# A Fourier layer with two mixtures on one Trainium2 core: where the small tiled products of a group stand, and the forward spectra's way to TensorE

## Chip, core and metric

The kernel runs on one NeuronCore of a Trainium2 chip. The metric is the device time of one execution in microseconds (us). The kernel before has a median of 1930.59 us over three runs (1930.12 to 1937.83).

## What is computed

Input x is 8 batches of 3072 tokens with 256 features. Three layers follow one another, all in fp32:

```
X = rfft(x, axis=1)                         # along the tokens
Yr = Xr @ w_r - Xi @ w_i + b_r ; Yi = Xr @ w_i + Xi @ w_r + b_i
Y = soft_threshold(Yr, 0.01) + 1j * soft_threshold(Yi, 0.01)
y = irfft(Y).reshape(24576, 256)
logits = y @ phi                            # 32 slots = 8 experts x 4
d = softmax(logits, axis=0) ; c = softmax(logits, axis=1)
slot_out[e] = relu((d.T @ y)[e] @ w1[e]) @ w2[e]
z = c @ slot_out
h = z @ w_in ; out = (h * tanh(softplus(h))) @ w_out      # 256 -> 2048 -> 256
```

## The kernel before

The work has two stages. The first, some 650 us, does the Fourier layer, the logits, both softmaxes and the sum of tokens into slots. The second runs the experts on 32 slots and then the last layer over all tokens; the diff doesn't touch it.

The transform is split in steps. Stage one (`stage1`, L186) multiplies a batch by a 64-point table in 64 x 64 tiles of the array and stores the result to DRAM (`sdr`, L216). `load_b` (L218) brings it back in another order, a quarter of a batch at a time: such a quarter is a group, 8 frequencies q of the 32, and 8 batches make 32 groups k. Stage two (`stage2`, L224, tile `s`, 32 products per group) finishes the spectrum and splits it into a high and a low part. `linear` (L247) does the complex product by the weights in six runs of six products (tile `l`: two feature halves `eh`, three partial sums `m`); behind each run with m > 0, VectorE adds (`p`), ScalarE makes two one-sided thresholds (`cl`, in one buffer, and `p`), and GpSimd subtracts them into `yt` (L285).

From yt, three things are made. `project` (L290, tile `pp`, in 32-column tiles of the array) multiplies by phi in the frequency domain. `inv1` (L301, tile `iu`, also 32-column tiles) starts the inverse transform of these logits. `ytrans` (L313, tile `tr`) transposes yt, twelve times a group, for the later sum into slots; its operand takes every sixth float of yt. Once a batch, the softmax chain follows: `sturn`, `inv2` (`lps`), `smax1` to `smax3` (`mt`, `mb`: a maximum over all tokens, spread by a product with a 32-row matrix of ones), `csoft1`, `cexp`, `csoft2`, `ctrans` (`ctps`). `fwd1` (L425, tile `dps`) transforms the exponentials forward; for all batches but the last it stores the result (`dm`) to DRAM (`ddr`), and `d_load` (L442) loads it back as `dd`. The last batch is turned on chip instead, by VectorE and eight transposes (`td`). `fwd2` (L472, tile `dt`, 32-column tiles) makes the spectra, `dturn` (L482) turns them, and `slots` (L487, tile `sps`, 32-column tiles) adds up the slots.

The order is written out as numbers. `at(position, function, ...)` collects calls; a position counts groups, so k + 0.5 lies in the middle of group k. The calls are sorted and issued in that order, on all engines, the DMA queue of SyncE among them. The dictionary `PA` (L798) holds the offsets: stage one's six pieces of a batch stand at 4b - 5.89 + 0.3402 j for j = 1, 3 to 11, `project` stands at k + 1.18, `inv1` at k + 1.48, `ytrans` at k + 2.24, stage two at k - 1.1, `load_b` at k - 1.91, and the chain of batch b at 4b + 4 plus its own offset.

All along, `conv` (L529) turns the last layer's weights from 64-bit to 32-bit floats in 32 pieces, on VectorE and GpSimd. The last batch has positions of its own (`TAIL`).

At the start, loads fill the time; 36 products `wm` on the identity matrix (`warm`, L520) run before the first stage two.

Of the kernel before, what the change touches and what calls it, by code (L numbers as in the profile page):

```python
# [31 lines left out]
def constants():  # L32

    n1 = np.arange(R1, dtype=np.float64)
    n2 = np.arange(R2, dtype=np.float64)
    f1 = np.zeros((R1, R1))
    t = np.zeros((96, NP, 96))
    w = 2.0 * np.pi / SEQ
    f1[:, 0], f1[:, 1] = 1.0, np.where(n1 % 2 == 0, 1.0, -1.0)
    for pos in range(47):  # L40
        k, r = (R1 * (pos + 1), 0) if pos < 23 else (R1 // 2 + R1 * (pos - 23), R2)
        a = w * np.mod(n2 * k, SEQ)
        t[r:r + R2, 0, pos] = np.cos(a)
        t[r:r + R2, 0, 48 + pos] = -np.sin(a)
    t[0:R2, 0, 47] = 1.0
    t[0:R2, 0, 95] = np.where(n2 % 2 == 0, 1.0, -1.0)
    for q in range(1, NP):
        ang = 2.0 * np.pi * np.mod(n1 * q, R1) / R1
        f1[:, 2 * q], f1[:, 2 * q + 1] = np.cos(ang), -np.sin(ang)
        for k2 in range(R2):  # L50
            a = w * np.mod(n2 * (q + R1 * k2), SEQ)
            sg = 1.0 if k2 < R2 // 2 else -1.0
            t[0:R2, q, k2] = np.cos(a)
            t[R2:96, q, k2] = np.sin(a)
            t[0:R2, q, 48 + k2] = -sg * np.sin(a)
# [13 lines left out]
def body(ctx, tc, x, w_r, w_i, b_r, b_i, phi, w1, w2, w_in, w_out, cbig, ct, out, dbg=None, stop=False):  # L69
# [39 lines left out]
    t_t = tall[:, NP * 144:].rearrange("p (n f) -> p n f", f=96)  # L109
    ones32 = const.tile([NS, 128], F32, name="ones32")  # L110
    s_acc = const.tile([128, D], F32, name="s_acc")
# [13 lines left out]
    x_t, b_t, xh_t, xl_t, yt_t, y_t, pt_t, k1_t = {}, {}, {}, {}, {}, {}, {}, {}  # L125
    sdr, spt, ddr, ch, a_t = {}, {}, {}, {}, {}
    XC = 512
# [96 lines left out]
    def stage2(k, h, p0):  # L224
# [17 lines left out]
        if g == 0 and p0 == 0:  # L242
            for t in (xh_t[k], xl_t[k]):
                nc.vector.tensor_copy(t[:, h, 3 * NC:3 * NC + 48].rearrange("p (a r) -> p a r", r=2),
                                      t[:, h, 95:144:48][:, None, :].to_broadcast([128, 24, 2]).bitcast(F32))

    def linear(k, eh, m):  # L247
        if eh == 0 and m == 0:
            pool, tag = (bp, "b") if k >= NK - 2 else (yq, "yq") if k >= NK - 4 else (ytp, "yt")
            yt_t[k] = pool.tile([128, 2, 8, 2, 48], F32, tag=tag, name="yt")  # L250
        xh, xl, yt = xh_t[k], xl_t[k], yt_t[k]
# [15 lines left out]
        if m == 0:  # L267
# [6 lines left out]
            return  # L274
        ri = m - 1
        p = lp.tile([128, 8, 48], F32, tag="p", name="p")
        nc.vector.tensor_add(p.rearrange("p q f -> p (q f)"), ps, k1_t[eh][:, 0:NC])  # L277
        cl = lp.tile([128, 8, 48], F32, tag="cl", bufs=1, name="cl")
        if k == NK - 1:
            nc.vector.tensor_scalar(cl, p, tlo[:, ri, eh:eh + 1], thi[:, ri, eh:eh + 1], op0=ALU.max, op1=ALU.min)  # L280
            nc.vector.tensor_sub(yt[:, eh, :, ri, :], p, cl)
        else:
            nc.scalar.activation(out=cl, in_=p, func=AF.Relu, bias=tup[:, ri, eh:eh + 1])  # L283
            nc.scalar.activation(out=p, in_=p, func=AF.Relu, scale=-1.0, bias=tlo[:, ri, eh:eh + 1])  # L284
            nc.gpsimd.tensor_sub(yt[:, eh, :, ri, :], cl, p)  # L285
# [67 lines left out]
    def smax2(b):  # L353
# [209 lines left out]

    def s1pos(b, j):
        if b < 2:
            return -5 + 0.05 * j if b == 0 else 0.15 + 0.195 * j
        if b == 2:
            return 2.5 + 0.305 * j
        return 4 * b + PA["s1"] + PA["s1d"] * j

# [4 lines left out]
    for b in range(NB):  # L575
        for i in range(na // 2):
            at(s1pos(b, 2 * i + 1), stage1, b, i)
        for i in range(na // 2 if b else 0):
            at(s1pos(b, 2 * i + 1.5), store_a, b, i)
            at(s1pos(b, 2 * i - 2.4) if i > 1 else s1pos(b - 1, 2 * i + 9.6) if b > 1 else -3.86 + 0.01 * i, load_x, b, i)  # L580
    for k in range(NK):
# [13 lines left out]
    for b in range(NB):  # L595
# [378 lines left out]
```

## Time and profile before

| | |
|---|---|
| median of three runs | 1930.59 us |
| the profiled execution | 1935.8 us |
| its span, first to last instruction | 1934.0 us |
| TensorE busy | 1875.3 us, 97% of the span |
| VectorE, ScalarE, GpSimd busy | 1163.1, 860.5, 195.3 us |
| chain that ended last, by engine | PE 88%, DMA 4%, DVE 3%, ACT 2% |
| moved by DMA | 164.28 MB in 96,905 packets, 28,784 of them under 512 bytes |

In the profile PE is TensorE's products, PEld its weight loads, DVE VectorE, ACT ScalarE, POOL GpSimd and SP SyncE. The ends of products are modelled, so starts are what to compare. A product in fp32 has two records, a transpose one, and an l product (rounded fp32) one.

### The profile page before, as it was taken

The page shows a single profiled execution, that of the slowest core. Times are in us where ns is not written, and L with a number is a line of the kernel's source. Part 1 is how long each engine was busy: PE and PEld are TensorE (multiplying, and loading weights), DVE is VectorE, ACT ScalarE, POOL GpSimd, SP SyncE. Part 2 cuts the span into 40 slices and gives each one's busy share as a digit, 9 for nine tenths or more (in the row PEclk, how much of TensorE's full clock was granted, in tenths as well). Part 3 has the DMA queues.
Part 4 walks back from the last instruction along what each step waited for, and adds up shares of the span by engine and source line. Part 5 has one row for each costly group of instructions (what it writes and reads, how often), then busy time and mean ns, then how long its engine had stood idle before and what let it go on. Part 6 is the DMA issues. An engine that isn't in the chain of part 4 may idle for free.

```text
span 1934.0 us, 29831 instructions
## 1 busy us (share of the span) xinstructions
PE 1875.3 (97%) x12106; PEld 1569.4 (81%) x12106; DVE 1163.1 (60%) x1810; ACT 860.5 (44%) x1380; POOL 195.3 (10%) x247
## 2 busy tenths in 40 slices
PE   6899999998998899999999999999999999999999
PEld 4687787777887488888888888888888888888887
DVE  3355655655566476666666666666666666666665
ACT  2666666665754243333333333333333333333332
POOL 0333333332332000000000000000000000000000
PEclk9999999999999999999999999999999999999999
DMA  9867777775663920020020020002002001000000
GB/s 246 235 150 173 168 184 177 170 185 132 161 167 107 343 74 22 23 55 22 12 55 23 23 55 23 23 12 55 22 23 55 22 19 48 22 23 22 23 22 23
DMA packets 96905, 164.28 MB, mean 85 GB/s; under 512 B 28784, under 2 KB 58096, under 8 KB 94848
## 3 DMA queue, kind: packets, MB, share of 16 engines
q1 hardware_dynamic: 93808, 155.13, 29.2%
q0 software_dynamic: 1792, 4.76, 0.8%
q10 hardware_dynamic: 1168, 2.49, 0.5%
q8 instruction: 95, 1.56, 0.3%
q14 instruction: 42, 0.34, 0.1%
HBM read 98.78 MB, written 63.57 MB: 84 GB/s over the span
## 4 chain that ended last, share of the span: by engine, by line
PE 88%; DMA 4%; DVE 3%; ACT 2%; issue 2%; POOL 1%; SPq 0%; POOLq 0%; ACTq 0%; DVEq 0%
PE o L910 56%; PE h L868 9%; PE l L265 8%; PE s L233 6%; PE tr L318 2%; PE s L201 2%; DMA dd<-ddr 2%; DMA bt<-sdr 1%; PE pp L296 1%; DMA xc<-in_x_dram 1%; PE sps L496 1%; POOL yt L285 1%; PE dt L478 1%; ACT cl L283 1%; PE iu L307 1%
## 5 line engine op out<-in xcount | busy, mean ns | idle before, releaser
L910 PE MATMUL o<-whl,gh 128*128 128x512 f32 x3072 | 1082.9, 395 | 0.0
L910 PE MATMUL o<-whl,gl 128*128 128x256 f32 x3072 | 827.9, 280 | 0.0
L881 ACT ACTIVATE g<-h 128x1024 f32<-128x1024 f32 (+1 forms) x385 | 394.2, 1025 | 747.8 <-PE h L868 738.0
L910 PEld LDWEIGHTS o<-whl,gh 128*128 128x128 f32 x3072 | 566.5, 188 | 121.5
L910 PEld LDWEIGHTS o<-whl,gl 128*128 128x128 f32 x3072 | 578.5, 188 | 31.5
L894 DVE TENSOR_TENSOR gl<-g,gh 128x1024 fp32r<-128x1024 f32 x383 | 468.9, 1224 | 29.2 <-DVE gh L887 1.4
L887 DVE CAST gh<-g 128x1024 fp32r<-128x1024 f32 (+1 forms) x385 | 265.8, 690 | 352.6 <-ACT g L881 352.6
L868 PE MATMUL h<-ctt,mst 128*128 128x512 f32 x768 | 240.7, 394 | 1.5 <-ACT g L881 1.0
L233 PE MATMUL s<-tall,bt 96*128 96x144 f32 x1024 | 143.0, 301 | 23.0 <-DMA bt<-sdr 12.1
L233 PEld LDWEIGHTS s<-tall,bt 96*128 96x128 f32 x1024 | 138.6, 202 | 31.0 <-issue 26.4
L241 DVE TENSOR_TENSOR xl<-s,xh 128x432 fp32r<-128x432 f32 (+1 forms) x192 | 94.6, 550 | 113.6 <-ACT xh L240 113.3
L285 POOL TENSOR_TENSOR yt<-cl,p 128x384 f32<-128x384 f32 x124 | 125.2, 1010 | 352.6 <-ACT p L284 220.2
L868 PEld LDWEIGHTS h<-ctt,mst 128*128 128x128 f32 x768 | 121.0, 188 | 19.7 <-ACT g L881 1.8
L283 ACT ACTIVATE cl<-p,tup 128x384 f32<-128x384 f32 x124 | 76.3, 615 | 134.0 <-DVE p L277 98.1
L918 DVE TENSOR_TENSOR os<-o,os 128x256 f32<-128x256 f32 x192 | 76.5, 419 | 77.2 <-ACT os L917 77.2
L277 DVE TENSOR_TENSOR p<-l,k 128x384 f32<-128x384 f32 x128 | 70.6, 553 | 85.2 <-PE l L265 61.9
L240 ACT ACTIVATE xh<-s 128x432 fp32r<-128x432 f32 (+1 forms) x192 | 79.0, 503 | 36.7 <-PE s L233 36.3
L917 ACT ACTIVATE os<-o 128x256 f32<-128x256 f32 x192 | 73.4, 383 | 41.5 <-PE o L910 37.7
L284 ACT ACTIVATE p<-p,tlo 128x384 f32<-128x384 f32 x124 | 76.3, 615 | 4.0
L201 PE MATMUL s<-xc,f 64*64 64x512 f32 x384 | 56.6, 650 | 9.6 <-DMA xc<-in_x_dram 9.5
L318 PEld LDWEIGHTS tr<-cb,yt 128*128 128x128 f32 x384 | 55.4, 235 | 12.0 <-issue 4.5
L318 PE MATMUL tr<-cb,yt 128*128 128x128 f32 x384 | 62.2, 306 | 0.0
(187 smaller groups left out, 1392.1 us busy)
## 6 DMA issues: line engine op xcount, KB each, us to landing
sdr<-a SPq DMA_DIRECT2D x96, 256.0 KB, 3.8
bt<-sdr SPq DMA_DIRECT2D x32, 768.0 KB, 8.5
out_dram<-os SPq DMA_DIRECT2D x47, 512.0 KB, 2.6
xc<-in_x_dram SPq DMA_DIRECT2D x90, 256.0 KB, 5.4
ctt<-c_d SPq DMA_DIRECT2D x28, 384.0 KB, 7.0
w1t<-in_moe_w_dram SPq DMA_DIRECT2D x6, 1024.0 KB, 7.4
c_d<-chl SPq DMA_DIRECT2D x14, 384.0 KB, 2.8
w2t<-in_moe_w_dram SPq DMA_DIRECT2D x5, 1024.0 KB, 12.2
```

The source lines that it names most:

```text
L201: nc.tensor.matmul(ps[h][64 * c:64 * c + 64], lhsT=f64[hs], rhs=t[hs, XC * c:XC * c + XC], start=True, stop=True, tile_position=(64 * h, 6 ...
L233: nc.tensor.matmul(ps[:, i], lhsT=b_t[k][:, p0 + i, h * 128:(h + 1) * 128], rhs=t_m[:, 8 * g + p0 + i, :], start=True, stop=True)
L241: nc.vector.tensor_sub(part(xl_t[k]), ps, xh.bitcast(F32))
L265: nc.tensor.matmul(full[:, 0:48 * nq].rearrange("p (q f) -> p q f", f=48), lhsT=ww[:, h, es], rhs=spec(xx, h), start=n == 0, stop=n == 5)
L283: nc.scalar.activation(out=cl, in_=p, func=AF.Relu, bias=tup[:, ri, eh:eh + 1])
L285: nc.gpsimd.tensor_sub(yt[:, eh, :, ri, :], cl, p)
L318: nc.tensor.transpose(ps[:, i, eh], yt[:, eh].rearrange("p q r f -> p (q r f)")[:, 2 * c + i::6], ident)
L868: nc.tensor.matmul(ps[:, i], lhsT=mst[:, f * 128:f * 128 + 128], rhs=ct_t[b][:, 4 * m:4 * m + 4].rearrange("p n t -> p (n t)"), start=True ...
L881: nc.scalar.activation(out=v(g), in_=v(h), func=AF.Mish)
L887: nc.vector.tensor_copy(v(gh), v(g))
L894: nc.vector.tensor_sub(gl, g, gh.bitcast(F32))
L910: nc.tensor.matmul(o, lhsT=a[:, i, ts], rhs=w, start=f == 0 and n == 0, stop=f == 15 and n == 1)
```

## The change

- yt gets the layout [feature half, 6, 128] instead of [half, 8, 2, 48], so that the 128 columns of one transpose lie side by side. GpSimd's subtraction now takes its inputs with a step of six floats and writes runs of eight. The inverse table's rows are permuted to fit.
- `inv1` moves from k + 1.48 to k + 2.179, just ahead of the next group's `project`. The whole chain of a batch moves about 0.7 group later, `slots` a whole one.
- Stage one gets new positions by hand, most at 0.175 of a group, just ahead of `inv1` and `project`; its store follows 0.17 later.
- `fwd2`'s four parts stand together, just ahead of `project`.
- All batches take the last batch's way for the spectra: `dm` is turned by VectorE, then by eight transposes `td`, and copied into one tile `dd`. The DRAM tensor `ddr`, its store and its load are gone.
- The matrix of ones has 128 rows instead of 32 in the product `mb`.
- Behind the warm-up, 26 more products (`filler`, 9728 columns) run on a weight tile.

```
-    tt = t.transpose(2, 1, 0)
+    r = np.arange(16)
+    tt = t.transpose(2, 1, 0)[np.concatenate([6 * r + m for m in range(6)])]
...
-    ones32 = const.tile([NS, 128], F32, name="ones32")
+    ones32 = const.tile([128, 128], F32, name="ones32")
...
+    def split6(t):
+        return t.rearrange("p q (f m) -> p m q f", m=6)
...
-            yt_t[k] = pool.tile([128, 2, 8, 2, 48], F32, tag=tag, name="yt")
+            yt_t[k] = pool.tile([128, 2, 6, 128], F32, tag=tag, name="yt")
...
+        o = yt[:, eh].rearrange("p m (q r f) -> p m q r f", q=8, r=2)[:, :, :, ri]
...
-            nc.gpsimd.tensor_sub(yt[:, eh, :, ri, :], cl, p)
+            nc.gpsimd.tensor_sub(o, split6(cl), split6(p))
...
-            v = yt[:, eh].rearrange("p q r f -> p q (r f)")
+            v = yt[:, eh].rearrange("p m (q j) -> p q m j", q=8)
...
-                nc.tensor.matmul(ps[32 * a:32 * a + 32], lhsT=ph[:, eh, :], rhs=v[:, :, 32 * a:32 * a + 32],
+                nc.tensor.matmul(ps[32 * a:32 * a + 32], lhsT=ph[:, eh, :], rhs=v[:, :, 2 * a:2 * a + 2],
...
-                nc.tensor.transpose(ps[:, i, eh], yt[:, eh].rearrange("p q r f -> p (q r f)")[:, 2 * c + i::6], ident)
+                nc.tensor.transpose(ps[:, i, eh], yt[:, eh, 2 * c + i], ident)
...
-            if last:
-                nc.vector.transpose(out=dm.rearrange("p q n -> p n q")[:, 12 * i:12 * i + 12], in_=ps)
-            else:
-                nc.scalar.activation(out=dm[:, 12 * i:12 * i + 12], in_=ps, func=AF.Copy)
-        if last:
-            ch[b, 0] = dm
-            return
-        ddr[b] = dram.tile([NP, 96, NS], F32, tag="ddr", bufs=2, name="ddr")
-        nc.sync.dma_start(out=ddr[b].rearrange("q (r n) s -> (q r) n s", r=4), in_=dm)
+            nc.vector.transpose(out=dm.rearrange("p q n -> p n q")[:, 12 * i:12 * i + 12], in_=ps)
+        ch[b, 0] = dm
...
         if b < NB - 1:
-            dd = cp.tile([96, NP, NS], F32, tag="dd", name="dd")
-            nc.sync.dma_start(out=dd, in_=ddr[b].rearrange("q p s -> p q s"))
-            ch[b, 0] = [dd[:, q] for q in range(NP)]
-            return
+            both = cp.tile([96, 2, 4, 128], F32, tag="dd", name="dd")
...
+    def filler():
+        ps = psum([128, 512], "wm")
+        w = wsp["a"][0]
+        for m, n, c in ((128, 512, 5), (127, 512, 5), (64, 512, 4), (128, 256, 4), (127, 256, 4), (128, 128, 4)):
+            for _ in range(c):
+                nc.tensor.matmul(ps[0:m, 0:n], lhsT=w[:, 0, 0:m], rhs=w.rearrange("p h e -> p (h e)")[:, 0:n], start=True, stop=True)
...
+    S1 = {0: [-4.95 + 0.1 * i for i in range(6)], 1: [0.475, 0.84, 1.175, 1.475, 1.84, 2.175], 2: [2.475, 3.175, 4.175, 4.475, 5.175, 5.475]}
+    for b in range(3, NB):
+        S1[b] = [4 * b + z for z in PA["s1"]]
...
-        at(k + PA["pj"] + 0.3, inv1, k)
+        at(k + PA["pj"] + (0.999 if k < NK - 1 else 0.3), inv1, k)
...
-            at(f2 + 0.1 * g if b < NB - 1 else NK + TAIL["f2"][g], fwd2, b, g)
+            at(f2 + 0.001 * g if b < NB - 1 else NK + TAIL["f2"][g], fwd2, b, g)
...
-PA = dict(y=20, s1=-5.89, s1d=0.3402, lb=-1.91, s2=-1.1, pj=1.18, yt=2.24, tu=0.482, i2=1.17, m1=1.17, m2=1.34, m3=1.51, f1=1.84, c1=1.58, ce=1.58, ds=2.47, dl=2.05, c2=2.57, f2=2.46, sl=3.2, cx=3.24, ...)
+PA = dict(y=20, s1=(-5.825, -4.825, -4.525, -3.825, -2.825, -2.525), lb=-1.91, s2=-1.1, pj=1.18, yt=2.24, tu=1.185, i2=1.87, m1=1.87, m2=2.04, m3=2.21, f1=2.52, c1=2.28, ce=2.28, ds=3.29, dl=2.88, c2=3.27, f2=3.176, sl=4.19, cx=3.95, ...)
```

What this does to the order shows at two places. On TensorE, around the forward spectra `dt` of batch 2, first before, then changed (of each run of six l products the first row stands):

```order
L201 MATMUL s_3349<-xc,f_120 64x512 x2
L201 MATMUL s_3350<-xc,f_120 64x512 x2
L478 MATMUL dt<-tall,dd 32x16x6 x8
L307 MATMUL iu<-tall,phat 32x96 x8
L265 MATMUL l<-xh,ah 128x384
...
L478 MATMUL dt<-tall,dd 32x16x6 x16
L265 MATMUL l<-xh,bh 128x384
...
L478 MATMUL dt<-tall,dd 32x16x6 x8
```

```order
L202 MATMUL s_3526<-xc,f_120 64x512 x2
L202 MATMUL s_3527<-xc,f_120 64x512 x2
L473 MATMUL dt<-tall,dd 32x16x6 x24
L312 MATMUL iu<-tall,phat 32x96 x8
L473 MATMUL dt<-tall,dd 32x16x6 x8
L301 MATMUL pp<-yt,ph 32x256 x6
L323 MATMUL tr<-cb,yt 128x128 x12
```

Where l products stood between three tiled pieces, one tiled stretch now holds stage one, all of dt, iu and the project that stood elsewhere; the transposes follow it.

On SyncE's queue, ahead of the first reload (`bt`) of batch 5, first before, then changed:

```order
L440 DMA ddr<-dm 128x768
L216 DMA sdr<-a 128x1x512 x2
L445 DMA dd<-ddr 96x32x32
L183 DMA xc<-in_x_dram 64x1024 x2
L221 DMA bt<-sdr 96x8x256
```

```order
L217 DMA sdr<-a 128x1x512 x2
L184 DMA xc<-in_x_dram 64x1024 x2
L535 DMA cvs<-in_moe_w_out_dram 128x512
L217 DMA sdr<-a 128x1x512 x2
L222 DMA bt<-sdr 96x8x256
```

The store and the load of the spectra stood around stage one's last store; now only loads of x, a load for the weight conversion (`cvs`) and stage one's stores stand ahead of the reload.

## Rows read from the trace of the kernel before

**Rows 1.** Windows, two stretches: us, busy us of each engine (instructions), clock, DMA share, GB/s.

```profile
100.00:600.00 500.00, 481.99 (x4008) 390.14 (x4008) 290.08 (x669) 327.73 (x674) 166.38 (x209) 0.98 0.64 161
680.00:1934.00 1254.00, 1249.97 (x6902) 1080.09 (x6900) 793.22 (x961) 462.15 (x576) 0.00 (x0) 1.00 0.10 30
```

**Rows 2.** Waits of TensorE, 28 to 620 us: who <- whom: us in total, times, longest.

```profile
PE s L233 <- DMA bt<-sdr: 12.1, 3, 6.5
PE dt L478 <- DMA dd<-ddr: 9.9, 7, 2.5
PE s L233 <- issue: 8.1, 2, 6.6
PE s L233 <- ACT dm L435: 2.5, 5, 0.9
```

**Rows 3.** Windows, six short stretches around waits.

```profile
30.00:42.00 12.00, 6.84 (x35) 6.87 (x36) 2.68 (x9) 2.61 (x6) 0.00 (x0) 0.72 1.04 226
90.00:104.00 14.00, 8.27 (x40) 8.30 (x41) 4.18 (x12) 4.20 (x10) 1.69 (x3) 0.63 0.91 235
390.00:398.00 8.00, 7.64 (x46) 6.81 (x46) 4.23 (x12) 4.62 (x9) 1.05 (x3) 0.79 0.64 157
466.00:476.00 10.00, 7.64 (x38) 7.61 (x38) 3.33 (x10) 4.13 (x8) 2.88 (x4) 0.66 0.80 194
537.00:545.00 8.00, 7.59 (x101) 6.36 (x102) 4.40 (x11) 2.57 (x5) 2.27 (x3) 0.79 1.06 328
605.00:613.00 8.00, 7.72 (x101) 6.50 (x102) 4.90 (x11) 2.95 (x5) 2.59 (x4) 0.79 0.05 18
```

**Rows 4.** Timeline of TensorE: start us, us, engine, line, op, out<-in, count [idle before].

```profile
35.16 10.61 PE L233 MATMUL s<-tall,bt 96*128 96x144 f32 x64 [6.62 <-issue]
...
239.97 0.87 PE L478 MATMUL dt<-tall,dd 96*32 96x96 f32 x32
240.77 0.45 PE L265 MATMUL l<-xh,bh 128*128 128x384 f32 x1
...
242.03 0.54 PE L478 MATMUL dt<-tall,dd 96*32 96x96 f32 x16
242.50 0.45 PE L265 MATMUL l<-xh,ch 128*128 128x384 f32 x1
...
255.58 0.49 PE L413 MATMUL ctps<-cb,lg 128*128 128x128 f32 x3
255.91 0.70 PE L318 MATMUL tr<-cb,yt 128*128 128x128 f32 x4
...
258.94 0.44 PE L265 MATMUL l<-xh,ah 128*128 128x384 f32 x1
...
261.27 1.09 PE L201 MATMUL s<-xc,f 64*64 64x512 f32 x8
...
263.46 4.08 PE L233 MATMUL s<-tall,bt 96*128 96x144 f32 x32
...
270.74 1.89 PE L318 MATMUL tr<-cb,yt 128*128 128x128 f32 x12
272.38 0.42 PE L265 MATMUL l<-xh,ch 128*128 128x384 f32 x1
```

**Rows 5.** Waits of SyncE's queue, 100 to 600 us.

```profile
SPq L440 <- ACT dm L435: 80.0, 7, 26.6
```

**Rows 6.** Groups of VectorE's instructions: xcount | busy us, mean ns | idle before.

```profile
L299 DVE STREAM_TRANSPOSE phat<-pp 96x256 f32<-96x256 f32 x32 | 14.1, 441 | 4.5 <-PE pp L296 4.4
...
L433 DVE STREAM_TRANSPOSE dm<-dps 128x384 f32<-128x384 f32 x2 | 2.1, 1152 | 0.2 <-PE dps L431 0.2
```

**Rows 7.** Timeline of ScalarE and of GpSimd, one group's thresholds.

```profile
274.37 0.61 ACT L283 ACTIVATE cl<-p,tup 128x384 f32<-128x384 f32 x1 [1.05 <-DVE p L277]
...
280.80 0.62 ACT L283 ACTIVATE cl<-p,tup 128x384 f32<-128x384 f32 x1 [1.12 <-POOL yt L285]
...
282.14 1.02 POOL L285 TENSOR_TENSOR yt<-cl,p 128x384 f32<-128x384 f32 x1 [1.37 <-ACT p L284]
```

More of the change, by code (lines that the diff above doesn't have):

```diff
@@ L125, in body @@
     x_t, b_t, xh_t, xl_t, yt_t, y_t, pt_t, k1_t = {}, {}, {}, {}, {}, {}, {}, {}
-    sdr, spt, ddr, ch, a_t = {}, {}, {}, {}, {}
+    sdr, spt, ch, a_t = {}, {}, {}, {}
     XC = 512
@@ L280, in linear @@
             nc.vector.tensor_scalar(cl, p, tlo[:, ri, eh:eh + 1], thi[:, ri, eh:eh + 1], op0=ALU.max, op1=ALU.min)
-            nc.vector.tensor_sub(yt[:, eh, :, ri, :], p, cl)
+            nc.vector.tensor_sub(o, split6(p), split6(cl))
         else:
@@ L284, in linear @@
             nc.scalar.activation(out=p, in_=p, func=AF.Relu, scale=-1.0, bias=tlo[:, ri, eh:eh + 1])
-            nc.gpsimd.tensor_sub(yt[:, eh, :, ri, :], cl, p)
+            nc.gpsimd.tensor_sub(o, split6(cl), split6(p))
         if m == 2 and k % 4 == 0:
             cs = cs_t.pop(eh)
-            nc.gpsimd.tensor_sub(yt[:, eh, 0, :, 47], cs[:, 0], cs[:, 1])
+            nc.gpsimd.tensor_sub(yt[:, eh, 5, 7:16:8], cs[:, 0], cs[:, 1])
     def project(k):
@@ L357, in smax2 @@
         nc.vector.tensor_reduce(mb, ps, axis=AX.X, op=ALU.max)
-        mdg = sm.tile([NS, NS], F32, tag="mdg", name="mdg")
-        nc.vector.tensor_scalar(mdg, ident[:NS, :NS], mb[:NS], SC, op0=ALU.mult, op1=ALU.mult)
+        mdg = sm.tile([128, NS], F32, tag="mdg", name="mdg")
+        nc.vector.tensor_scalar(mdg, ident[:, :NS], mb, SC, op0=ALU.mult, op1=ALU.mult)
         nc.vector.tensor_scalar(mb, mb, SC, None, op0=ALU.mult)
@@ L427, in fwd1 @@
         last = b == NB - 1
-        dm = cp.tile([128, 32, N2] if last else [128, N2, NS], F32, tag="st" if last else "chl", bufs=1 if last else 2, name="dm")
+        dm = cp.tile([128, 32, N2], F32, tag="st" if last else "chl", bufs=1 if last else 2, name="dm")
         for i in range(2):
@@ L453, in d_load @@
                 nc.tensor.transpose(ps[:, c], src[:, 4 * a + c], ident)
-            dd = yp.tile([96, 4, 128], F32, tag="y", name="dd")
+            dd = both[:, a] if b < NB - 1 else yp.tile([96, 4, 128], F32, tag="y", name="dd")
             if a:
@@ L516, in weight_sum2 @@
         ps = psum([128, NS], "wb")
-        nc.tensor.matmul(ps, lhsT=ones32, rhs=ch["wd"], start=True, stop=True)
+        nc.tensor.matmul(ps, lhsT=ones32[:NS], rhs=ch["wd"], start=True, stop=True)
         nc.vector.tensor_mul(ch["w"], sel, ps)
@@ L562, in view @@
                 [dst[128 * h:128 * h + 128, CW * i:CW * (i + 1)] for h in range(r // 128) for i in range(c // CW)])
[L564 to L569, printed above, removed]
+    S1 = {0: [-4.95 + 0.1 * i for i in range(6)], 1: [0.475, 0.84, 1.175, 1.475, 1.84, 2.175], 2: [2.475, 3.175, 4.175, 4.475, 5.175, 5.475]}
+    for b in range(3, NB):
+        S1[b] = [4 * b + z for z in PA["s1"]]
     at(-9, setup)
@@ L576, in body @@
         for i in range(na // 2):
[L577 to L580, printed above, removed]
+            at(S1[b][i], stage1, b, i)
+            if b:
+                at(S1[b][i] + 0.17, store_a, b, i)
+                at(S1[b][i - 2] + 0.06 if i > 1 else S1[b - 1][4 + i] + 0.06 if b > 1 else -3.86 + 0.01 * i, load_x, b, i)
     for k in range(NK):
@@ L600, in body @@
         for g in range(4):
-            at(f2 + 0.1 * g if b < NB - 1 else NK + TAIL["f2"][g], fwd2, b, g)
-            at(f2 + 0.1 * g + 0.15 if b < NB - 1 else NK + TAIL["dt"][g], dturn, b, g)
+            at(f2 + 0.001 * g if b < NB - 1 else NK + TAIL["f2"][g], fwd2, b, g)
+            at(f2 + 0.11 + 0.001 * g if b < NB - 1 else NK + TAIL["dt"][g], dturn, b, g)
         if b < NB - 2:
@@ L623, in body @@
     at(-4.2, warm, 36)
+    at(-4.15, filler)
     at(NK + TAIL["ws"], weight_sum)
@@ L795, in run @@
                 nc.vector.tensor_copy(sot[:, h, 16 * g:16 * g + 16].rearrange("p (j i) -> p j i", i=SPE), src)
-PA = dict(y=20, s1=-5.89, s1d=0.3402, lb=-1.91, s2=-1.1, s2d=0.0002, pj=1.18, yt=2.24, ytd=0.0002, tu=0.482, i2=1.17, m1=1.17, m2=1.34, m3=1.51, f1=1.84, c1=1.58, ce=1.58, ds=2.47, dl=2.05, c2=2.57, f2=2.46, sl=3.2, rc=0.3, cx=3.24, cxd=0.0002, x0=-0.79, x1=0.05, ytl=1.05, x2=1.3, x3=2.7)
+PA = dict(y=20, s1=(-5.825, -4.825, -4.525, -3.825, -2.825, -2.525), lb=-1.91, s2=-1.1, s2d=0.0002, pj=1.18, yt=2.24, ytd=0.0002, tu=1.185, i2=1.87, m1=1.87, m2=2.04, m3=2.21, f1=2.52, c1=2.28, ce=2.28, ds=3.29, dl=2.88, c2=3.27, f2=3.176, sl=4.19, rc=0.3, cx=3.95, cxd=0.0002, x0=-0.79, x1=0.05, ytl=1.05, x2=1.3, x3=2.7)
 TAIL = {
```

## The prediction

> **What bounds the kernel now.** I read the windows by stage first. From 680 us on TensorE is busy 1250.0 of 1254 us at full clock, and the change touches nothing there, so only the first 680 us can move. Between 100 and 600 us TensorE is busy 482.0 of 500 us, while VectorE has 290, ScalarE 328 and GpSimd 166 [rows 1]: TensorE is the bound of this stage too, and a nanosecond that it no longer needs is a nanosecond of the kernel, unless another wait ends later. Then the waits of TensorE between 28 and 620 us: 12.1 us for the reloads of stage one's result (bt), 9.9 us for the spectra's way back from DRAM (dd, seven times), 2.5 us for the dm copies, 8.1 us put down to issue, of which 6.6 once [rows 2]. Last the granted clock around those waits: in six stretches the mean lies between 0.63 and 0.79, a mix of the two levels, 1.2 and 2.4 GHz [rows 3]. Each stretch holds a wait before or inside it, and the products behind the wait run at the low level.
>
> **The change part by part.**
>
> *Stays in a tiled mode.* Six l products between two stays take 1.26 us (240.77 to 242.03), twelve in a row between two stays 2.33 (258.94 to 261.27). Two sixes therefore cost 0.19 us more than a twelve. Thirty-two dt records take 0.80 us until the next l starts and sixteen 0.47, so sixteen cost 0.33 and the end of each stay in column tiles a fixed 0.14 [rows 4]. By the order of both programs, from the first s product to the experts, stays fall from 115 to 54, column-tiled stretches from 83 to 38, and runs of l from 131 to 92. Column tiles: 45 x 0.14 = 6.3 us. The l side: between 39 x 0.19 = 7.4 (runs that vanish) and 61 x 0.19 = 11.6 (stays that vanish); many stays border on tr or s products instead of l. Together 13.7 to 17.9 us; I take **15**, nearer the count of runs. Stage one, whose tiles are 64 by 64, gets no gain of its own for standing beside iu: I count the end of its stay as before.
>
> *Unit-stride transposes.* Today yt is read with a step of six floats. Twelve such transposes take 1.64 us (270.74 to 272.38), 137 ns each; three of ctps, whose operand is contiguous, take 0.33 us (255.58 to 255.91), 110 ns each [rows 4]. 384 x 27 ns = **10** us less. The bounds are nothing (if the place in the stream made the difference) and these 10; the row of the same engine doing the same operation on contiguous data is the nearest, so I take it.
>
> *Spectra on chip.* Seven batches get eight more transposes (td): 56 x 110 ns = **6** us more on TensorE. VectorE gets two strided transposes of 1.15 us (the last batch already does this [rows 6]) and a copy per batch, and is idle 42% of this stage [rows 1]; ScalarE swaps two copies for one. Cover on the way: twelve l products (2.33 us) and half of dps between dps and td, against 2.3 us of VectorE, whose queue may be behind; I book 2 us of new waits. Between td and dt stand stage two and twelve l, which cover the two copies. The DRAM round trip goes, and with it the 9.9 us of dd and the 2.5 us of dm [rows 2].
>
> *SyncE's queue.* The ddr store waited 80.0 us in total at the head of SyncE's queue [rows 5], with stage one's stores behind it and the bt load behind those. Now nothing of the spectra stands there, and the last stage-one piece of a batch comes 0.377 group earlier in the order (4b-2.525 for 4b-2.148). The c_d stores still wait there, but directly ahead of a bt load that is not the first of its batch. Of bt's 12.1 us, 6.5 is one wait at 95.7 us, in the stretch that DMA fills (its share is 0.91 at 90 to 104 us [rows 3]); I take 2 off that and drop the other **5.6**. The smaller of the two issue waits, 8.1 - 6.6 = 1.5 us, is bt number 3, issued two stage-one pieces later than it will be: dropped. Sum for DMA waits: 9.1.
>
> *Clock.* Half-clock time is twice the missing share times the window; half of what was worked in it was lost. 30 to 42 us: 0.28 x 12 = 3.4, less 0.8 for the part in which nothing ran, 2.6. The filler is 9728 columns of the kind of l; twelve l products are 4608 columns in 2.33 us [rows 4], so it takes about 4.9. It runs in the idle 6.6 us behind the warm-up (28.54 to 35.16), in which the level fell, and should keep it up. It ends 1.7 us before stage two can start, so it costs nothing; at the low level throughout it would end 3.2 us too late. Around 392, 470, 540 and 608 us: 1.7 + 2.7 + 1.7 + 1.7 [rows 3], gone with the waits ahead of them. Together 10.4, taken as **10**. The 3 us around 97 us stay.
>
> *GpSimd.* Its subtraction now reads its two inputs with a step of 24 bytes. Without such a row here I bound it: 1.02 us as now [rows 7], or 1.02 x 1.74 = 1.77, by VectorE's strided 1.152 us for 384 elements against 0.441 for 256 contiguous ones, 0.662 for as many [rows 6]. I take 1.4, the middle. The cover: cl has one buffer, so a group's yt are a chain, each from a cl (280.80) to the end of yt (282.14 + 1.02), 2.36 us, that is 1.34 and the subtraction P [rows 7]. The first cl starts 2.0 us after the transposes end (274.37 [rows 7] against 272.38); three links end at 2.0 + 3 x 1.34 + 3P = 6.0 + 3P us. TensorE is back at project after a stage-one piece with six l (2.19 us, 261.27 to 263.46), thirty more l (2.5 x 2.33 = 5.8) and stage two (4.1): 12.1 us [rows 4]. P = 1.4 leaves 1.9 us. GpSimd's conversion pieces stand in that chain in some groups, so I book **4** us of waits in all.
>
> The GPSIMD Engine Reference of the Trainium skill (section 7, performance pitfalls) states that reading SBUF with a step over 8 bytes costs about 50% more per element; by it P would be some 1.5 us, an estimate, and the sum would stand. No row here shows such a read.
>
> *inv1 a group later, and with it the softmax chain.* One group more of y tiles waits for slots: six groups of three, 18 of 20 buffers; the other waits keep their distances. Nothing. The tail has the same order from its transposes on. Nothing.
>
> **Sum**, against the profiled execution's own 1935.8 us: TensorE 15 + 10 - 6 = 19; dd and dm 12.4; DMA waits 9.1; clock 10; together 50.5. New waits: GpSimd 4, td 2, and 4 more, an estimate, for the clock behind these and for loads that come no earlier in the first 100 us. Gain 40.5, time 1895. The profiled execution was 5 us over the median 1930.6, and waits for loads, which vary, are what I remove; against the median I give **1893**.
>
> **Rivals.**
> *The loads do not follow.* TensorE is faster, but bt and xc land as late as now, and the bt waits and their clock stay or grow. For it: DMA's share is 0.64 from 100 to 600 us [rows 1] and 0.91 at 90 to 104 [rows 3]. Against: dd and ddr go, and SyncE is freed. Then 19 + 12.4, less 10 new waits and 5 of clock: gain 16, 1915 on the median. Chance 0.17.
> *The stays cost the same.* If stage one's and the column-tiled mode drained as before and only l runs merged, 15 becomes 5: 1903. Chance 0.1.
> *GpSimd becomes the bound (slower).* At P = 2.03 the chain equals TensorE's 12.1 us; from there each 0.1 costs 0.3 us in each of 31 groups, 9 us. At 2.5 the gain is eaten; at 2.7 it is 0.67 x 3 x 31 = 62 us: 1893 - 4 + 62 = 1951. Against: both bounds from rows lie below 2.03. Chance 0.05.
> *More comes.* No new waits and all bt waits gone: 1935.8 - 57 = 1879. Chance 0.08.
>
> **How the numbers follow.** The forecast, 1884 to 1903, has 0.58; the rest is 0.02 for no change. About 0.5%, 10 us, is what a measurement of this kernel can tell from no change. Faster by more than that needs under 1921: forecast, more, equal stays and nearly all of the load case, 0.9; same 0.05; slower 0.05. Range 1878 to 1916: it leaves out the slower case, the no-change case and the edges of the others.
>
> **What would show it.** tr twelve at about 1.32 us from start to start; one stay with dt, iu and pp per batch; no dd wait, bt waits only near 85 us; full clock from 33 us to 80 and from 100 to 600; yt on GpSimd between 1.0 and 1.8 us and project's wait for it under 10 us in total. I am wrong if project waits for yt in most groups, if td or dt waits more than 1 us a batch, or if bt waits appear at the start of most batches.

## The result and the profile after

The changed kernel takes 1960.16 us (median, 1957.31 to 1961.11) beside 1930.36 us for the kernel before in the same comparison: a ratio of 1.0135, 95% interval 1.0116 to 1.0154. It is 1.35% slower. The forecast was 1893 us, 2% faster, with 0.05 for slower; the prediction was wrong, in sign too.

The page of the changed kernel, its head and the busy times:

```profile
span 1955.5 us, 29971 instructions
...
PE 1874.6 (96%) x12188; PEld 1572.4 (80%) x12188; DVE 1191.3 (61%) x1831; ACT 853.8 (44%) x1373; POOL 274.3 (14%) x247
...
L290 POOL TENSOR_TENSOR yt<-cl,p 128x384 f32<-128x384 f32 x124 | 201.4, 1624 | 302.9 <-ACT p L289 190.3
```

GpSimd's subtraction takes 1624 ns where it took 1.02 us [rows 7]. Next the windows of the changed kernel, the first the same as in [rows 1], the second inside the last layer:

```profile
100.00:600.00 500.00, 463.03 (x3990) 378.22 (x3990) 305.34 (x666) 311.53 (x646) 228.21 (x203) 0.99 0.59 151
700.00:1950.00 1250.00, 1250.00 (x6900) 1080.31 (x6898) 791.96 (x957) 461.03 (x574) 0.00 (x0) 1.00 0.10 30
```

The last layer keeps TensorE busy without a gap, as before. The loss lies ahead of it: between 100 and 600 us TensorE is busy 463.0 us, 19 less than before [rows 1]. It has less to do and waits more. The timelines of both kernels give the size: the first product of stage two and the first of the experts (`hp`), in the kernel before

```profile
35.16 3.22 PE L233 MATMUL s<-tall,bt 96*128 96x144 f32 x12 [6.62 <-issue]
...
651.36 4.00 PE L761 MATMUL hp<-w1t,sit 128*32 128x512 f32 x20 [1.05 <-DVE sit L648]
```

and in the changed kernel

```profile
36.32 1.95 PE L234 MATMUL s<-tall,bt 96*128 96x144 f32 x14 [1.38 <-issue]
...
671.20 3.46 PE L761 MATMUL hp<-w1t,sit 128*32 128x512 f32 x16 [1.05 <-DVE sit L648]
```

From the one to the other it was 616.2 us and is 634.9: 18.7 more. The trace's idle times of TensorE between these two starts add up to 27 us more than before. The waits of TensorE from 28 to 620 us, as in [rows 2]:

```profile
PE l L269 <- DVE xl L242: 14.4, 8, 3.6
PE s L234 <- DMA bt<-sdr: 6.4, 2, 4.9
PE l L269 <- DVE rm L348: 6.0, 5, 2.9
PE s L202 <- DVE xl L242: 5.2, 5, 2.0
PE tr L323 <- ACT a L208: 3.3, 5, 0.8
PE td L448 <- DVE dm L437: 3.1, 3, 1.5
```

The waits for the load `dd` and for ScalarE's copies `dm` are gone, and those for `bt` have halved. In their place the l products wait for VectorE's `xl`, the second half of stage two's eviction, and for `rm`, the last reader of the logits' PSUM tile. By the program's order the `xl` waited for belongs to the next group, and `rm` is no operand of an l product at all: what they wait for is a free PSUM buffer. Both readers stand behind an eviction by ScalarE (`xh`, `lg`). What ScalarE itself waits for, 100 to 640 us, in the changed kernel

```profile
ACT cl L288 <- DVE p L282: 86.8, 51, 4.5
ACT cl L288 <- POOL yt L290: 69.5, 47, 2.3
```

and in the kernel before:

```profile
ACT cl L283 <- POOL yt L285: 27.2, 25, 1.5
```

One place shows how the two hang together. ScalarE of the changed kernel, around stage two and `ctps` of batch 2:

```profile
336.69 0.62 ACT L288 ACTIVATE cl<-p,tup 128x384 f32<-128x384 f32 x1 [0.74 <-DVE p L282]
337.34 0.62 ACT L289 ACTIVATE p<-p,tlo 128x384 f32<-128x384 f32 x1
339.66 0.62 ACT L288 ACTIVATE cl<-p,tup 128x384 f32<-128x384 f32 x1 [1.70 <-POOL yt L290]
340.31 0.61 ACT L289 ACTIVATE p<-p,tlo 128x384 f32<-128x384 f32 x1
340.83 2.37 ACT L241 ACTIVATE xh<-s 128x432 fp32r<-128x432 f32 x6
```

GpSimd's subtraction, which frees `cl`:

```profile
338.05 1.57 POOL L290 TENSOR_TENSOR yt<-cl,p 128x384 f32<-128x384 f32 x1
```

TensorE:

```profile
335.75 4.08 PE L234 MATMUL s<-tall,bt 96*128 96x144 f32 x32
339.67 0.82 PE L418 MATMUL ctps<-cb,lg 128*128 128x128 f32 x6
342.03 0.46 PE L269 MATMUL l<-xh,ah 128*128 128x432 f32 x1 [1.54 <-DVE xl L242]
```

The last `cl` of the group stands 1.70 us until the subtraction of the one ahead of it has read the only buffer (338.05 + 1.57). From one `cl` to the next it is 2.97 us, which is the prediction's 1.34 + P with P = 1.62. ScalarE takes its instructions in order, so the six `xh` behind it begin at 340.83, 5.1 us after stage two began to fill PSUM. Stage two's six tiles and the two of `ctps` are then the eight buffers that the kernel has, and the next l product, at 342.03, waits 1.54 us for the first of them. Waits of this kind add up to 25.6 us in the lines above (14.4 + 6.0 + 5.2); the kernel before has none of the three.

The granted clock falls behind such waits. Three of them, for `xl`, are 2.02, 2.99 and 3.58 us long and end at 363.41, 496.93 and 575.54 us; in the windows around them the level is 1.2 GHz for a part, which makes the mean 0.83:

```profile
360.00:370.00 10.00, 7.98 (x61) 4.93 (x61) 7.46 (x13) 6.04 (x15) 2.96 (x4) 0.83 0.20 52
494.00:504.00 10.00, 7.08 (x69) 5.17 (x73) 5.73 (x13) 7.44 (x17) 4.01 (x5) 0.83 0.37 118
572.00:582.00 10.00, 6.46 (x70) 5.22 (x74) 6.34 (x15) 6.48 (x15) 3.68 (x4) 0.83 0.29 94
```

The low stretches of [rows 3] around 392, 470 and 540 us are gone; these are new ones.

### The profile page after: what moved, and what is told of

Same layout as the page of the kernel before. It is cut to its first block, busy times and chain, and to the rows that moved or that the text cites. A ratio compares the mean times of both kernels' runs of the same rounds, so it can differ in the third digit from the quotient of the medians.

```text
span 1955.5 us, 29971 instructions
## 1 busy us (share of the span) xinstructions
PE 1874.6 (96%) x12188; PEld 1572.4 (80%) x12188; DVE 1191.3 (61%) x1831; ACT 853.8 (44%) x1373; POOL 274.3 (14%) x247
## 3 DMA queue, kind: packets, MB, share of 16 engines
q8 instruction: 96, 1.57, 0.3%
## 4 chain that ended last, share of the span: by engine, by line
PE 66%; DVE 2%; ACT 1%; POOL 1%; issue 1%; POOLq 0%; ACTq 0%; DVEq 0%
PE o L910 55%; PE h L868 9%; POOL yt L290 1%; PE hp L761 0%; PE so L776 0%; DVE xl L242 0%; PE l L269 0%; ACT cl L288 0%; ACT p L289 0%; PE dt L473 0%; DVE p L282 0%; PE pp L301 0%; PE tr L323 0%; PE sps L491 0%; DVE dh L479 0%
## 5 line engine op out<-in xcount | busy, mean ns | idle before, releaser
L881 ACT ACTIVATE g<-h 128x1024 f32<-128x1024 f32 (+1 forms) x385 | 394.2, 1025 | 749.2 <-PE h L868 740.4
L290 POOL TENSOR_TENSOR yt<-cl,p 128x384 f32<-128x384 f32 x124 | 201.4, 1624 | 302.9 <-ACT p L289 190.3
L234 PE MATMUL s<-tall,bt 96*128 96x144 f32 x1024 | 134.9, 291 | 7.8 <-DMA bt<-sdr 6.4
L234 PEld LDWEIGHTS s<-tall,bt 96*128 96x128 f32 x1024 | 132.4, 194 | 11.8 <-ACT p L289 5.2
L202 PE MATMUL s<-xc,f 64*64 64x512 f32 x384 | 66.4, 680 | 18.0 <-DMA xc<-in_x_dram 11.8
L269 PE MATMUL l<-xh,ah 128*128 128x384 f32 (+1 forms) x128 | 50.1, 392 | 20.7 <-DVE xl L242 13.6
L328 ACT ACTIVATE y<-tr 128x512 f32<-128x512 f32 x93 | 48.8, 600 | 19.5 <-PE tr L323 19.5
```

The source lines that it names most:

```text
L234: nc.tensor.matmul(ps[:, i], lhsT=b_t[k][:, p0 + i, h * 128:(h + 1) * 128], rhs=t_m[:, 8 * g + p0 + i, :], start=True, stop=True)
L290: nc.gpsimd.tensor_sub(o, split6(cl), split6(p))
L881: nc.scalar.activation(out=v(g), in_=v(h), func=AF.Mish)
```

## The experiments

Three theories were set against each other. **G**: GpSimd's slower subtraction stretches the chain through the single `cl` buffer, ScalarE evicts later, TensorE waits for PSUM. **O**: the new order does it, above all VectorE's work that now stands in one lump (`csoft2` and four `dh`) ahead of an add `p`. **S**: the spectra's strided transposes on VectorE do it. All the results, sorted by ratio; the kernel before ran beside each of them, with medians of 1930.36 to 1933.73 us:

| kernel | median us | ratio to before, 95% interval |
|---|---|---|
| changed kernel | 1960.16 | 1.0135 (1.0116 to 1.0154) |
| a_c2: csoft2 later | 1957.35 | 1.0126 (1.0106 to 1.0147) |
| b_layout: before, layout alone | 1957.66 | 1.0123 (1.0100 to 1.0145) |
| b_table: before, layout and permuted table | 1927.78 | 0.9968 (0.9952 to 0.9985) |
| a_cl2: two buffers for cl | 1924.40 | 0.9959 (0.9940 to 0.9979) |
| a_table_nofill: permuted table, no filler | 1926.05 | 0.9954 (0.9939 to 0.9969) |
| a_table: permuted table | 1922.52 | 0.9940 (0.9925 to 0.9955) |
| b_chip: before, spectra on chip alone | 1917.54 | 0.9917 (0.9897 to 0.9936) |
| a_cl2_c2_conv: a_t2_c2_conv without the table | 1909.93 | 0.9887 (0.9870 to 0.9904) |
| a_t_c2_conv: a_t2_c2_conv with one buffer | 1909.78 | 0.9884 (0.9869 to 0.9900) |
| b_table_chip: b_table and spectra on chip | 1906.34 | 0.9851 (0.9823 to 0.9879) |
| a_table_cl2: table and two buffers | 1903.59 | 0.9835 (0.9803 to 0.9867) |
| b_table_chip_cl2: b_table_chip, two buffers for cl | 1900.94 | 0.9834 (0.9817 to 0.9851) |
| a_t2_c2: table, two buffers, csoft2 later | 1896.56 | 0.9811 (0.9792 to 0.9830) |
| a_t2_c2_conv: and the conversion spread | 1893.79 | 0.9799 (0.9780 to 0.9818) |

### The subtraction made fast again (a_table)

The six parts of yt want every sixth frequency. That order can be had for nothing if the columns of the forward table stand in it: then the spectrum, the l products and the thresholds carry it along, and GpSimd reads contiguous rows.

```
+    t = t.reshape(96, NP, 2, 8, 6).swapaxes(3, 4).reshape(96, NP, 96)
     t3 = np.concatenate([t[:, :, 0:48] + t[:, :, 48:96], t], axis=2)
...
-        return t.rearrange("p q (f m) -> p m q f", m=6)
+        return t.rearrange("p q (m f) -> p m q f", m=6)
...
-   nc.tensor.matmul(... .rearrange("s m n -> s n m"), lhsT=dd[q], rhs=t_m[:, q, 48:144].rearrange("p (n m) -> p n m", m=6), ...
+   nc.tensor.matmul(... .rearrange("s m (r f) -> s r m f", r=2), lhsT=dd[q], rhs=t_m[:, q, 48:144].rearrange("p (r m f) -> p r m f", r=2, m=6), ...
```

> The changed kernel with the columns of the forward table permuted, so that the spectrum leaves stage two already in the order of yt's six parts: GpSimd's subtraction reads contiguous rows again and still writes runs of eight; nothing else moves. Theory G (GpSimd's slower subtraction, 1.62 us for 1.01, stretches the chain through the single cl buffer; ScalarE, which works in order, evicts stage two's and the logits' tiles later, and TensorE waits for free PSUM): yt falls to 1.0 to 1.2 us, ScalarE's waits of cl for yt from 69 us to about 30 us, and 15 to 27 us come back: 1933 to 1945. Theory O (the order: VectorE's burst of csoft2 and four dh ahead of p, iu and pp and stage one side by side): yt falls as well, but the time stays over 1952. Theory S (the spectra's strided transposes on VectorE): over 1952 too.

Measured: 1922.52 us, 38 less than the changed kernel, more than any theory asked for. GpSimd's group of yt, 100 to 600 us:

```profile
L291 POOL TENSOR_TENSOR yt<-cl,p 128x384 f32<-128x384 f32 x111 | 113.8, 1025 | 276.2 <-ACT p L290 162.5 <-PE tr L324 86.8 <-ACT a L209 8.0
```

Writing runs of eight costs nothing that can be seen (1025 ns); the strided reads cost all of it. O and S fall as the main cause. ScalarE's wait behind GpSimd is 37.2 us in this kernel, half of the changed kernel's.

### The coupling taken away, the subtraction left slow (a_cl2)

```
-        cl = lp.tile([128, 8, 48], F32, tag="cl", bufs=1, name="cl")
+        cl = lp.tile([128, 8, 48], F32, tag="cl", bufs=2, name="cl")
```

> The changed kernel with two buffers for cl in place of one; the subtraction stays as slow. G in its narrow form (only the single buffer couples GpSimd's time to ScalarE): ScalarE's wait of cl for yt falls from 69 us to under 20 us, 1935 to 1945. If GpSimd is late by its own sum as well (project then waits for yt): 1945 to 1955. O and S: within 5 us of 1960.

Measured: 1924.40 us, 36 less, and under the range of the narrow form. GpSimd is as slow as in the changed kernel, 1637 ns; project still does not wait for it. ScalarE at the place shown above:

```profile
328.48 0.62 ACT L289 ACTIVATE p<-p,tlo 128x384 f32<-128x384 f32 x1
329.06 0.62 ACT L288 ACTIVATE cl<-p,tup 128x384 f32<-128x384 f32 x1
329.71 0.62 ACT L289 ACTIVATE p<-p,tlo 128x384 f32<-128x384 f32 x1
330.23 2.38 ACT L241 ACTIVATE xh<-s 128x432 fp32r<-128x432 f32 x6
```

TensorE there:

```profile
327.01 4.08 PE L234 MATMUL s<-tall,bt 96*128 96x144 f32 x32
330.93 0.82 PE L418 MATMUL ctps<-cb,lg 128*128 128x128 f32 x6
331.50 0.45 PE L269 MATMUL l<-xh,ah 128*128 128x432 f32 x1
```

The last `cl` follows at once, `xh` begins 3.2 us after stage two instead of 5.1, and the l product behind `ctps` has no wait. So at this place it was not that GpSimd is late with yt, but that it keeps ScalarE standing. The mechanism of G's narrow form is there; that the single buffer is the only way from the slow subtraction to TensorE is not shown, and a_table_cl2 below speaks against it.

### Each part by itself on the kernel before (b_layout, b_chip)

b_layout is the kernel before with the diff's lines on yt and tt alone, b_chip with its lines of `fwd1` and `d_load` alone.

> The kernel before with nothing but the new layout of yt (strided reads on GpSimd, unit-stride transposes, table rows permuted). The twelve transposes give 11 us back. G: yt takes 1.6 us here too, and what TensorE waits for rises by 15 us or more: 1930 to 1945. O and S: nothing follows from the slower subtraction at the old places: 1917 to 1922.

> The kernel before with nothing but the spectra turned on chip (VectorE's strided transposes, eight td a batch, no DRAM way). S: VectorE's 2.3 us a batch and the copies delay p, 1935 to 1950. G and O: the waits for dd (9.9 us) and dm (2.5 us) go, 6 us of transposes come: 1922 to 1930.

Measured: 1957.66 and 1917.54 us. The layout alone makes the old order slower by 25 us, beyond the range that G was given, though its transposes give back 10. The waits of TensorE in b_layout:

```profile
PE dt L483 <- DMA dd<-ddr: 12.9, 7, 3.6
...
PE s L234 <- ACT dm L440: 6.7, 6, 1.6
PE lps L345 <- DVE xl L242: 5.0, 3, 2.8
PE mt L360 <- DVE rm L355: 4.4, 5, 2.0
PE pp L301 <- POOL yt L290: 3.4, 1, 3.4
```

ScalarE's copies (`dm`, and through them the way to DRAM and back), `xl` and `rm` come late in this order too; the harm does not need the new order. The spectra on chip are a gain of 15 us by themselves, more than the range given for them, and S falls. The `bt` wait in b_chip:

```profile
PE s L233 <- DMA bt<-sdr: 6.5, 1, 6.5
```

It was 12.1 [rows 2]: the 5.6 us that the prediction put down to SyncE's queue came exactly.

### Do the parts add up, and what is the order worth (b_table, b_table_chip, a_table_cl2, a_table_nofill)

b_table is b_layout with the table of a_table; b_table_chip has the spectra on chip too; a_table_cl2 joins a_table and a_cl2; a_table_nofill is a_table without the line that calls `filler`.

> The kernel before with the new layout of yt and the permuted forward table: unit-stride transposes, and GpSimd reads contiguous rows. If the strided read is the whole harm of the layout, yt takes 1.03 us, the 11 us of the transposes come, and the time is 1932 - 11 = 1921 (1918 to 1925). If writing runs of eight, or the new reads of project, harm as well: over 1928.

> As the run before this one, and with the spectra on chip: everything of the change except its order, the wider matrix of ones and the filler. If the parts add up, 1932 - 11 - 15 = 1906 (1902 to 1910). Theory O then reads: the new order costs what the changed kernel with the permuted table (1922.5) lies above this, 12 to 20 us. If the new order is worth something, this run lies over 1922.

> The changed kernel with the permuted table and two buffers for cl. If ScalarE's remaining waits behind GpSimd (37 us) still hold up TensorE: 1908 to 1916. If what is left comes from VectorE's queue (the burst ahead of p) and from the order: 1919 to 1924, as with either alone.

> The changed kernel with the permuted table, without the 26 filler products. The prediction gave the filler 2.6 us through the clock at the start: 1925. If the low stretch only moves to another place (in the changed kernel it lies behind 42.9 us): 1921 to 1923.5. If the filler delays the first stage two (36.3 us against 35.2): 1921 or less.

Measured: 1927.78, 1906.34, 1903.59 and 1926.05 us. b_table missed: the transposes are 11 us shorter in its trace, but only some 6 us reach the end. The wait for `dd` there is 14.3 us instead of 9.9, so part of what TensorE saves it spends at the DRAM way, where it now arrives earlier. Against b_layout it is 30 us: the strided reads cost that in the old order too. With the DRAM way gone (b_table_chip) the sum is what was expected.

a_table_cl2 lies under both of its ranges. With the changed kernel, a_table and a_cl2 it closes a square. The slow subtraction costs 38 us with one buffer and 21 with two; the single buffer costs 36 us at the slow subtraction and 19 at the fast one. So some 17 us need both, and 21 of the slow subtraction's 38 us remain without the single buffer.

The filler's 2.6 us can't be told from nothing: the intervals of a_table and a_table_nofill overlap. It does hold the clock where it was meant to: from 30 to 42 us the granted clock is 1.00 with it and 0.72 without. From 68 to 80 us it is the other way round, 0.72 and 1.00, so a low stretch stands at another place.

### VectorE's lump, and a kernel that beats both (a_c2, b_table_chip_cl2, a_t2_c2, a_t2_c2_conv)

```
-PA = dict(... c2=3.27, ...)
+PA = dict(... c2=3.45, ...)
```

and, in the last of the four only,

```
-                cv[t] = cvp.tile([128, n], I32, tag="c" + t, name="cv" + t)
+                cv[t] = cvp.tile([128, n], I32, tag="c" + t, bufs=2 if t == "c" else 1, name="cv" + t)
...
-            at(c0 + sp * (i + st / 9), conv, s_, d_, ii, st)
+            at(c0 + sp * (i + (st + 2 * (st > 2)) / 9), conv, s_, d_, ii, st)
```

> The changed kernel with csoft2 at 3.45 instead of 3.27, so that VectorE does it behind the add p of the first half's last run, in the 3.3 us before the next add is due; the layout and the single cl buffer stay. Theory G (GpSimd's slow subtraction through the cl buffer and ScalarE's order): the burst is only a part, one group in four, 1950 to 1957. Theory O (the order, and in it this burst): 1935 to 1945.

> The kernel before with the permuted table, the spectra on chip and two buffers for cl: all but the order, the wider ones and the filler, with ScalarE freed from GpSimd. In the old order TensorE hardly waits for anything behind cl (its waits there sum to some 5 us), so 1900 to 1906 where the run without the second buffer gave 1906. The new order (1903.6 with both) then is worth nothing net: its 16 us of TensorE work are eaten by waits. If this run lies over 1910, the order is worth more than thought.

> The changed kernel with the permuted table, two buffers for cl and csoft2 at 3.45. If the waits that are left in the new order come from VectorE's burst ahead of p (6.3 us behind ctps, 6.1 us of l for xl): 1894 to 1900. If p is late for another reason (VectorE waits for the conversion's product on GpSimd): 1901 to 1904.

> As the run before this one; besides, the conversion's third to sixth step come 2/9 of a piece later and its tile cvc has two buffers, so that VectorE does not stand and wait for GpSimd's product (waits of 1.8 to 2.5 us ahead of p). If these waits matter on the path: 3 to 6 us under the run without it, 1888 to 1897. If they are covered: the same within 2 us.

b_table_chip_cl2 is b_table_chip with two buffers for `cl`; a_t2_c2 is a_table_cl2 with `csoft2` moved.

Measured: 1957.35, 1900.94, 1896.56 and 1893.79 us. In the changed kernel the lump is worth 2 to 3 us, within the intervals of both, which puts a_c2 at the upper edge of G's range and far from O's; with ScalarE freed, moving `csoft2` gives 5 to 7, by intervals that overlap. The last step gives 2.8 us more, within the intervals of both. The old order with the table, the spectra on chip and two buffers stands at 1900.94 us, no slower than the new order with the same mends (a_table_cl2, 1903.59); with `csoft2` moved the new order is some 4 us ahead, again by overlapping intervals. The conversion was not spread in the old order. Windows of a_t2_c2_conv:

```profile
100.00:600.00 500.00, 490.48 (x4503) 410.24 (x4506) 341.53 (x763) 341.65 (x700) 177.95 (x216) 1.00 0.64 176
```

Its waits of TensorE, 28 to 620 us, the four longest:

```profile
PE s L235 <- DMA bt<-sdr: 6.0, 2, 4.6
PE s L203 <- DMA xc<-in_x_dram: 2.5, 1, 2.5
PE pp L302 <- DVE yt L287: 2.4, 1, 2.4
PE dps L437 <- ACT dx L390: 1.9, 2, 1.0
```

TensorE is busy 490.5 of 500 us with a granted clock of 1.00, and what it waits for longest are loads in the first 100 us and the tail.

### The two halves of the loss, once more apart (a_cl2_c2_conv, a_t_c2_conv)

The first is a_t2_c2_conv without the permuted table, the second is a_t2_c2_conv with one buffer for `cl`.

> The changed kernel with its slow subtraction (strided reads), two buffers for cl, csoft2 at 3.45 and the conversion's steps apart: the run at 1893.8 without the permuted table. With the old places of csoft2 and the conversion, the slow subtraction still cost 21 us in spite of two buffers (1924.4 against 1903.6). If that went through VectorE's queue (it waits for GpSimd's product of the conversion, and the adds p behind it come late): 1895 to 1902. If VectorE's operations themselves run longer beside GpSimd, or the chain is late by its own sum: 1908 to 1916.

> The same with the permuted table and one buffer for cl. With the old places the one buffer cost 19 us at the fast subtraction (1922.5 against 1903.6). If ScalarE's wait for GpSimd costs so much only because VectorE's late add stands in the same chain: 1896 to 1902. If the single buffer costs it by itself: 1908 to 1914.

Measured: 1909.93 and 1909.78 us. Each half costs 16 us by itself, and moving `csoft2` and the conversion's steps, which come ahead of VectorE's adds, took neither away. The single buffer holds ScalarE at the fast subtraction too: cl waits 39.6 us for yt in a_t_c2_conv. With two buffers the slow subtraction still costs 16 us, though `cl` waits only 5.2 us for yt in a_cl2_c2_conv and project 0.2 us. What the traces offer for that is a longer time of VectorE's own instructions beside it (last section): from the first stage two to `hp` VectorE is busy 391.4 us there and 370.2 us in a_t2_c2_conv, with as many instructions. That this is the way to TensorE is argued, not shown.

## Why the prediction was wrong, step by step

**The step that failed is the cover of GpSimd's subtraction**: "P = 1.4 leaves 1.9 us", and from it 4 us of waits. The price was sound: 1.62 us lies between the bounds of 1.02 and 1.77, and the link of 1.34 + P was measured at 2.97 us. Even the prediction's own formula stays quiet: 6.0 + 3 x 1.62 = 10.9 us is less than 12.1. (It was short of its own rows: at P = 1.02 it gives 9.1 us, and from 272.38 [rows 4] to the end of the last yt, 283.16 [rows 7], it was 10.8, since the links also wait for VectorE's `p`.) But it asked when **project** needs yt, and project is not the first to suffer. The consumer that mattered is the engine in the middle of the chain. While ScalarE stands at `cl`, everything in its queue stands too, and stage two's and the logits' evictions are in that queue. Their deadline is PSUM's eight buffers, a few microseconds off, not 12.1. The part of [rows 7] that said so was in the prediction: its second row is ScalarE's own wait of 1.12 us for yt, and with P up by 0.6 us in each link it could only grow. Project's wait for GpSimd, the sign that the prediction named, is not among TensorE's waits in the changed kernel. The step booked 4 us of waits; the runs put 38 us on the slow subtraction (a_table) and 36 on the single buffer (a_cl2), and 57 on both together (a_table_cl2), of the 67 us between forecast and result. How 21 of the 38 reach TensorE stays open.

**The rival "GpSimd becomes the bound"** had the right side and the right engine, at 0.05, but its point of decision was wrong: P = 2.03 at project, where 1.62 at ScalarE was enough.

The Trainium skill, GPSIMD Engine Reference, section 7 (performance pitfalls), gives about 50% more per element for reads with a step over 8 bytes, which made P some 1.5 us as an estimate. The traces have 1.02 us [rows 7] and 1624 ns, 59% more. The rule holds in kind and is a little low for this instruction with two strided inputs.

**TensorE's own terms were right.** Twelve `tr` take, from start to start in the changed kernel, 1.26 us:

```profile
157.22 1.51 PE L323 MATMUL tr<-cb,yt 128*128 128x128 f32 x12
158.48 0.43 PE L269 MATMUL l<-xh,ch 128*128 128x384 f32 x1
```

against the 1.64 of [rows 4]; 1.32 was forecast. For the rest I took the steps from start to start of all TensorE's runs between the first stage two and `hp`, less the idle times and half of the time at the low clock. In a_table_cl2, where ScalarE is free, that is 20.7 us less than before: `tr` 11.6 less, `td` 6.1 more, and everything else, the stays in tiled modes, 15.2 less. Forecast were 10, 6 and 15. So "the stays cost the same" falls as a price of TensorE's work. In the changed kernel the same account leaves 4.4 us for the stays; the rest went into short stops inside its runs, 6.6 us in stage one's alone.

**The order's own waits** are a second step that failed. The prediction put them at nothing ("the other waits keep their distances. Nothing"). Between the same two starts TensorE is idle for 30.3 us in a_table_cl2 and for 13.8 us in b_table_chip_cl2, the old order with the same mends and without the filler. These 16.5 us eat what the stays gave: the two kernels take 1903.59 and 1900.94 us, which their intervals do not tell apart.

**The waits for DMA** went nearly as forecast: no `dd` and no ScalarE `dm`, and `bt` at 6.4 us where the sum left 4.5. "The loads do not follow" could not show in a kernel that is slower; it falls by a_t2_c2_conv, where TensorE is as fast as forecast and waits 6.0 us for `bt`.

**The clock's 10 us** did not come in the changed kernel, because new waits put new low stretches in place of the old ones. In a_t2_c2_conv the stretch from 100 to 600 us is at 1.00 instead of 0.98 [rows 1]. The term was right only on the condition that no wait takes the old one's place, and the sum did not carry that condition. For the filler, no gain was shown.

**The waits booked for `td`**, 2 us, were 3.1. **VectorE's lump** was not in the sum: the prediction looked at VectorE's load (idle 42%) and at the place of `td`, not at what the move puts ahead of the next add. It cost 5 to 7 us with the rest mended, by intervals that overlap.

With the failed step mended in two places (the permuted table, a second buffer) and the lump moved, the kernel lands at 1896.6 and, with the conversion spread, 1893.8 us. That is where the forecast was, but in part by luck. The sum had no term for the second buffer, which brings some 5 us in the old order too (1906.34 to 1900.94, by overlapping intervals), nor for the conversion's spread; and it had none for the order's waits, of which a_t2_c2_conv still holds some.

## What to carry to other kernels

When an instruction on an idle engine gets slower, don't ask only when its result is needed; ask who stands still until it frees its inputs, and what is queued behind that one. A chain through a single buffer binds an in-order engine to the slowest link, and the price appears where that engine's other work has its deadline, here in PSUM evictions. If the new order of an array can be put into a constant table at the start of the pipeline, no engine has to pay for the strides.

## What the runs showed of the hardware that was not expected

VectorE and GpSimd lengthen each other. In the changed kernel VectorE's two-input step of the conversion takes 0.41 us ahead of a subtraction and 1.80 us beside one:

```profile
337.67 0.41 DVE L548 SCALAR_TENSOR_TENSOR cva<-cvs,cva 128x256 int32<-128x256 int32 x1
...
484.52 1.80 DVE L548 SCALAR_TENSOR_TENSOR cva<-cvs,cva 128x256 int32<-128x256 int32 x1
```

and that subtraction takes 2.03 us instead of 1.57:

```profile
484.01 2.03 POOL L290 TENSOR_TENSOR yt<-cl,p 128x384 f32<-128x384 f32 x1 [6.72 <-PE tr L323]
```

Over the first 650 us this step takes 0.42 us on the mean in the 21 cases in which GpSimd computes during less than a quarter of it, and 1.18 us in the 7 with a subtraction beside more than a quarter. A slower subtraction lies in the way longer. The subtraction of `csoft1` on VectorE in a_cl2_c2_conv (strided reads on GpSimd)

```profile
L397 DVE TENSOR_TENSOR lg<-lg,cm 128x768 f32<-128x768 f32 x7 | 11.5, 1647 | 0.2
```

and in a_t2_c2_conv (contiguous reads), where nothing else differs:

```profile
L398 DVE TENSOR_TENSOR lg<-lg,cm 128x768 f32<-128x768 f32 x7 | 7.6, 1090 | 0.2
```

The adds `p`, which read one input from PSUM, keep their 553 ns in both. The Trainium skill, GPSIMD Engine Reference, section 8 (key points), says that the two engines share SBUF interfaces and contend when a VectorE instruction runs in a 2-port perf mode or has two SBUF inputs; these rows, all of instructions with two inputs, agree. The cast of `xl` (L245), which has one input, takes 1.54 us beside a subtraction, at 99.71 us of the changed kernel, and 0.18 us with nothing beside it; whether it runs in such a mode no trace shows.
